# Values of both groups of a query tile together, ahead of the flip of P, in a fused attention and soft mixture-of-experts kernel

## The chip, the core and the metric

The kernel runs on one core of one Trainium2 chip. The metric is the device time of one execution in microseconds (us). Five engines work beside each other, each through its own instruction stream in order: PE (TensorE, matrix products, with its weight loads listed as PEld), DVE (VectorE), ACT (ScalarE), POOL (GpSimd) and SP, which here only issues DMAs. They meet at semaphores alone.

## The reference, cut to what matters

```python
def _attn_ref(q, k, v):                     # q, k, v: 8 x 8 heads x 576 x 64, fp32
    window = 128
    scores = 0.125 * q @ k.T
    scores = where((rel >= 0) & (rel < window), scores + slope_h * -abs(rel), -1e9)
    attn = exp(scores - max(scores)); attn = attn / (sum(attn) + 1e-9)
    return attn @ v

x = attn_out.transpose(0, 2, 1, 3).reshape(4608, 512)
logits = x @ phi                            # 4608 x 32 slots
d = softmax of logits over the tokens;  slot_input = d.T @ x
per expert (8): h = relu(slot_input @ w1[e]); slot_out = h @ w2[e]
c = softmax of logits over the slots;   out = c @ slot_out
```

## The kernel before, in words

The program has an attention part, in which the logits and the running sums of the slots are taken along, and after it the expert part. The change lies in the attention part.

**Groups and rounds.** A batch has five query tiles `t`: four of 128 rows and a tail of 64. A full tile is worked on in two groups `g` of four heads each, the tail in one of all eight, so a batch has nine groups, and there are 72 in all (`groups`). The loop `for i in range(n)` at L770 runs one round for each. Round `i` brings each of several groups one step on; for group `i` the scores are masked and reduced on DVE and go through `exp`, for group `i - 1` the result is normalised, and so on:

- `scores(i + 1)` on PE (L248 and L255, or L236 and L241 for the first tile of a batch) writes one of two PSUM banks, which `expo(i - 1)` has to have read;
- `softmax_front` on DVE: `merge` (L268, L270 or L272), `rowmax` (L290), the reciprocal for the group before (L302), `bias` (L293) and four `normalise` (L307);
- `expo` on ACT (L342): four exponentials with their row sums, into one of three buffers `p4`; it waits for the bias;
- `flip` of group `i - FLAG`, which is `i - 3`, on PE (L352): four transposes of P into the PSUM bank `pt`;
- `split` of the same group: ACT copies `pt` to SBUF (L359), and POOL cuts the copy with two selects into the part of the tile before (`pp`) and that of this tile (`pd`) (L361 and L363, for the tail L366 and L368; for the first tile of a batch there is none);
- `values` of group `i - LAG`, which is `i - 4`, on PE (L388): P times V into the PSUM bank `xp`, in which both groups of a tile meet;
- behind the second group of a tile `after_values`: ACT copies `xp` to SBUF (`x_store`, L404). `x_flip` (four transposes on PE, L409, bank `xq`) and `x_keep` (the copy of `xq` on ACT, L418) follow some rounds later.

`pd` and `pp` have two buffers each, so the copy of a group's `pt` waits for the values of the group two before it. `pt`, `xp` and `xq` have one PSUM bank each.

**What sets the order.** The order on each engine is the order in which the program issues, since the schedule is manual. `do(when, i, ...)` (L693) puts a step off to round `i` and to a place in it, and `run(when, i)` carries it out: "act" stands behind the split, "mid" and "pe" behind the scores. The steps of the slots (`logits`, `slot_flip`, `token_flip`, `slot_sum` on PE, the copies and exponentials to them on ACT) are put off in this way and lie in rounds 4 to 8 of each nine. Names such as round 0 or 3 below mean the round's number modulo 9. Since a group's values follow four rounds behind, the second group's values of the full tiles come in rounds 5, 7, 0 and 2, and the tail's in round 3.

**On PE a round before reads** scores, an `x_flip` where there is one, the flip of P, the values, and the next scores. These products use the array in different shapes: flips 128x128, values 128x64 (tail 64x64), scores 64x32 (64x128 in the first tile), logits and slot sums 128x32. On ACT a round before reads: the copy of `pt`, that of `xq`, that of `xp`, and four exponentials.

## Time and profile before

| | |
|---|---|
| median of 3 runs | 292.06 us (291.81 to 293.53) |
| profiled execution, its own time | 291.1 us |
| its span, first to last instruction | 289.4 us |
| granted TensorE clock, mean | 0.981 |
| PE busy | 273.0 us, 94% |
| PE weight loads busy | 191.7 us, 66% |
| DVE busy | 232.7 us, 80% |
| ACT busy | 204.0 us, 71% |
| POOL busy | 92.2 us, 32% |
| HBM traffic | 71.7 MB, 248 GB/s |

The profile is one execution. The rounds of the attention part fill about 16 to 222 us of the span, the expert part what follows. In a row of the timeline stand the start (us from the span's start), the time it takes, the engine, the source line, the operation, the tile written and read, shapes, a count, and in brackets the idle time of the engine ahead of it with what ended it. A PEld row is a run of weight loads, two for each fp32 product; the loads pace the products, and the gap between two PEld rows shows best where PE waits. "issue" means that nothing the profile shows ended the idle time.

### The profile page before, as it was taken

The numbers are of one execution on the slowest core, as the hardware profiler recorded it, in microseconds if no ns is written. First come the engines' busy times: TensorE is split into PE (matmuls) and PEld (weight loads), VectorE is DVE, ScalarE is ACT, GpSimd is POOL, SyncE is SP. The second block draws the span as 40 slices with busy tenths as digits, with TensorE's granted clock in tenths as the row PEclk, the third lists the DMA queues.
The fourth block names the chain that finished last, engine by engine and source line by source line (L and its number), as shares of the span: only waits on it lengthen the run. The fifth ranks groups of instructions, "written<-read, shape, count | busy, mean of one in ns | idle before, by whom it ended". The sixth has DMA issues, their size and how long they took to land.

```text
span 289.4 us, 13086 instructions
## 1 busy us (share of the span) xinstructions
PE 273.0 (94%) x5164; PEld 191.7 (66%) x5164; DVE 232.7 (80%) x729; ACT 204.0 (71%) x811; POOL 92.2 (32%) x206
## 2 busy tenths in 40 slices
PE   7399999999999999999999999999999999999981
PEld 4267777777677767776777677757777753576640
DVE  2899999999989999988999999979999533234451
ACT  2798898987988988979798887978886431023341
POOL 2025525541544244235424450634465001000000
PEclk9699999999999999999999999999999999999997
DMA  6644478978686888777777968675648779999896
GB/s 183 218 143 115 130 204 254 290 215 279 188 278 196 292 272 261 236 231 229 230 243 245 302 208 279 225 261 172 199 160 272 244 251 351 416 418 356 333 383 273
DMA packets 35025, 72.58 MB, mean 251 GB/s; under 512 B 4210, under 2 KB 15124, under 8 KB 34964
## 3 DMA queue, kind: packets, MB, share of 16 engines
q1 hardware_dynamic: 34244, 71.24, 74.2%
q8 instruction: 41, 0.67, 0.9%
q10 hardware_dynamic: 720, 0.51, 0.5%
q14 instruction: 20, 0.16, 0.2%
HBM read 62.29 MB, written 9.44 MB: 248 GB/s over the span
## 4 chain that ended last, share of the span: by engine, by line
PE 50%; DVE 40%; issue 3%; ACT 2%; POOL 1%; DMA 1%; ACTq 0%; DVEq 0%; POOLq 0%
DVE area L307 14%; DVE s L290 10%; PE xp L388 9%; DVE s L270 5%; PE pt L352 5%; PE op L947 5%; PE hp L911 5%; PE s L255 5%; PE po L968 4%; DVE s L268 3%; PE xq L409 3%; PE s L248 2%; PE lp L427 2%; PE ap L510 1%; ACT area L342 1%
## 5 line engine op out<-in xcount | busy, mean ns | idle before, releaser
L342 ACT ACTIVATE area<-s,nb 128x128 f32<-128x128 f32 x288 | 102.2, 373 | 22.0 <-DVE nb L293 20.9
L307 DVE TENSOR_SCALAR area<-area,rs 128x128 f32<-128x128 f32 x286 | 79.4, 339 | 0.6 <-DVE nb L293 0.3
L388 PE MATMUL xp<-area 128*64 128x128 f32 (+1 forms) x1104 | 75.2, 271 | 1.1 <-DMA area<-v_n 0.2
L388 PEld LDWEIGHTS xp<-area 128*64 128x64 f32 x1104 | 56.2, 136 | 16.1 <-issue 8.6
L342 ACT ACTIVATION_READ_ACCUMULATOR area<-s,nb 128x1 f32 x288 | 60.7, 211 | 0.0
L290 DVE TENSOR_REDUCE s<-s 128x4 f32<-128x512 f32 x71 | 49.5, 697 | 2.2
L359 ACT COPY area<-pt 128x512 f32<-128x512 f32 x70 | 41.9, 598 | 10.1 <-PE pt L352 9.8
L298 POOL TENSOR_SCALAR rs<-sm 128x4 f32<-128x4 f32 x70 | 13.7, 195 | 100.5 <-ACT area L342 99.7
L352 PE MATMUL pt<-unit_r,area 128*128 128x128 f32 x284 | 45.6, 283 | 0.0
L255 PE MATMUL s<-kq 64*32 64x160 f32 x1792 | 42.2, 303 | 0.0
L352 PEld LDWEIGHTS pt<-unit_r,area 128*128 128x128 f32 x284 | 31.9, 142 | 14.3 <-PE s L255 5.0
L361 POOL TENSOR_SCALAR_AFFINE_SELECT area<-area 128x512 f32<-128x512 f32 x48 | 31.2, 650 | 24.8 <-ACT area L359 22.9
L270 DVE COPY_PREDICATED s<-cst,s 128x512 f32<-128x512 int32 x48 | 32.9, 685 | 0.2 <-PE s L255 0.2
L363 POOL TENSOR_SCALAR_AFFINE_SELECT area<-area 128x512 f32<-128x512 f32 x48 | 31.4, 654 | 3.3
L255 PEld LDWEIGHTS s<-kq 64*32 64x32 f32 x1792 | 29.7, 108 | 0.6
L248 PE MATMUL s<-ramp,ones 64*32 64x320 bf16 x448 | 18.8, 311 | 5.5 <-ACT area L342 4.9
L974 DVE COPY ob<-po 128x384 f32<-128x384 f32 x24 | 12.3, 552 | 14.2 <-PE po L968 12.0
L409 PE MATMUL xq<-unit_r,area 128*128 128x128 f32 x136 | 22.0, 285 | 0.4
L404 ACT COPY area<-xp 128x512 f32<-128x512 f32 (+1 forms) x37 | 20.9, 564 | 1.9 <-PE xp L388 1.5
L418 ACT COPY area<-xq 128x512 f32<-128x512 f32 x34 | 20.7, 610 | 0.0
L974 ACT COPY ob<-po 128x384 f32<-128x384 f32 x24 | 10.3, 481 | 12.8 <-PE po L968 12.8
L409 PEld LDWEIGHTS xq<-unit_r,area 128*128 128x128 f32 x136 | 14.5, 141 | 6.2 <-issue 3.2
(167 smaller groups left out, 310.2 us busy)
## 6 DMA issues: line engine op xcount, KB each, us to landing
w<-w SPq DMA_DIRECT2D x53, 512.0 KB, 5.3
out<-ob SPq DMA_DIRECT2D x24, 384.0 KB, 4.1
kq<-q_t SPq DMA_DIRECT2D x69, 128.0 KB, 3.2
kq<-k_t SPq DMA_DIRECT2D x32, 256.0 KB, 4.1
area<-v_n SPq DMA_DIRECT2D x31, 256.0 KB, 4.4
area<-w SPq DMA_DIRECT2D x8, 512.0 KB, 4.5
area<-v_n SPq DMA_DIRECT2D x12, 128.0 KB, 3.1
kq<-w SPq DMA_DIRECT2D x3, 512.0 KB, 6.2
```

The source lines that it names most:

```text
L248: nc.tensor.matmul(s4[32 * c:32 * c + 32, 2 * par:2 * par + 2, 32 * r:32 * r + WIN], lhsT=ones[rows, 0:32], rhs=ramp[rows, h], start=True, ...
L255: nc.tensor.matmul(s4[32 * c:32 * c + 32, 2 * par + jj, 32 * r:32 * r + WIN], lhsT=qt[rows, 2 * h + jj if t == 4 else jj, 32 * r:32 * r + 32],
L270: nc.vector.copy_predicated(s4[:, :, P:2 * P], bc(mask_u, 1, 4), s4[:, :, 0:P])
L290: nc.vector.tensor_reduce(st[key]["mx"][:, us], merged(key, us), axis=AX.X, op=ALU.max, negate=True)
L307: mul(p4[:, u], p4[:, u], st[key]["rs"][:, u:u + 1])
L342: nc.scalar.activation(s["p4"][:, u], merged(key, u), AF.Exp, bias=s["nb"][:, u:u + 1], scale=SCALE, accum_out=s["sm"][:, u:u + 1],)
L352: nc.tensor.transpose(s["pt"][:, u], s["p4"][:, u], ident)
L359: copy(pa[:, us], s["pt"][:, us])
L361: nc.gpsimd.affine_select(pp[:, us], pa[:, us], [[0, m], [-1, P]], ALU.is_gt, 0.0, base=0, channel_multiplier=1)
L363: nc.gpsimd.affine_select(pa[:, us], pa[:, us], [[0, m], [1, P]], ALU.is_ge, 0.0, base=0, channel_multiplier=-1)
L388: nc.tensor.matmul(xp[D * par:D * par + D, j, 0:w], lhsT=v_slot[b, t - 1 + ph][0:rows, D * h:D * h + D], rhs=src[:, 2 * par + i] if t < 4 ...
L409: nc.tensor.transpose(xq[:, P * j:P * j + P], x_of(b, t)[:, j], ident)
```

## The change

Three things move, and nothing is added or left out.

1. The values of a tile's two groups are issued together, in the round in which the second one's were issued before. A round that closes a tile ("closing", rounds 5, 7, 0, 2 and 3) issues both groups' values, or the tail's one; the other rounds (6, 8, 1 and 4) issue none.
2. These values, and the copy of `xp` with all else in `after_values`, stand at the beginning of that round, in front of the flip of P and its copy.
3. An `x_flip` that stood behind the scores of the round behind the closing one stands there directly behind the flip of P, in front of the scores, except for some (the tiles 0 and 2 of batches 2, 4 and 6, tile 1, and the last batch).

```diff
+    def closes(key):
+        return key[2] == 1 or key[1] == 4
+
     def after_values(i, key):
         b, t, g = key
-        if not (g == 1 or t == 4):
-            return
...
-            do("pe", i + 1 + (p == 1 and late), x_flip, b, t)
+            near = b < last and (p == 3 or p in (0, 2) and not late)
+            do("flip" if near else "pe", i + 1 + (p == 1 and late), x_flip, b, t)
...
+            if i >= LAG and closes(groups[i - LAG]):
+                b, t, g = groups[i - LAG]
+                for key in [(b, t, h) for h in range(g + 1)]:
+                    values(key)
+                after_values(i, groups[i - LAG])
             if i >= FLAG:
                 flip(groups[i - FLAG])
                 split(groups[i - FLAG])
             run("act", i)
-            if i >= LAG:
-                values(groups[i - LAG])
-                after_values(i, groups[i - LAG])
+            run("flip", i)
             if i + 1 < n:
                 scores(i + 1)
...
+        values(groups[n - 5])
+        values(ga)
         token_copy(last)
         x_keep(last, 2)
         flip(gb)
...
         normalise(gd, ALL)
-        values(ga)
```

The instruction order shows it at three places. On PE, rounds 35 and 36 (numbers 8 and 0 modulo 9), from the slot sum (L510) to the scores of group 37, before:

```order
L510 MATMUL ap<-area,dn 32x512 x4
L352 MATMUL pt<-unit_r,area 128x128 x4
L388 MATMUL xp<-area 64x128 x8
L236 LDWEIGHTS ones
L236 MATMUL s_0_83<-ramp,ones 128x2x128
L236 LDWEIGHTS ones
L236 MATMUL s_0_83<-ramp,ones 128x2x128
L241 MATMUL s_0_83<-kq 128x128 x4
L409 MATMUL xq<-unit_r,area 128x128 x4
L352 MATMUL pt<-unit_r,area 128x128 x4
L388 MATMUL xp<-area 64x128 x8
```

The same place in the changed kernel:

```order
L510 MATMUL ap<-area,dn 32x512 x4
L352 MATMUL pt<-unit_r,area 128x128 x4
L236 LDWEIGHTS ones
L236 MATMUL s_0_83<-ramp,ones 128x2x128
L236 LDWEIGHTS ones
L236 MATMUL s_0_83<-ramp,ones 128x2x128
L241 MATMUL s_0_83<-kq 128x128 x4
L409 MATMUL xq<-unit_r,area 128x128 x4
L388 MATMUL xp<-area 64x128 x16
L352 MATMUL pt<-unit_r,area 128x128 x4
```

The eight values (L388) behind the first flip are gone to the next round, which has sixteen, and they stand ahead of its flip (L352).

On PE, round 39 (number 3), where the tail's values are due, between two scores, before:

```order
L248 LDWEIGHTS ones
L248 MATMUL s_1_84<-ramp,ones 32x2x160
L255 MATMUL s_1_84<-kq 32x160 x16
L352 MATMUL pt<-unit_r,area 128x128 x4
L388 MATMUL xp<-area 64x64 x16
L248 LDWEIGHTS ones
```

And in the changed kernel, the flip of the tail (round 38) now being ahead of the first rows:

```order
L248 LDWEIGHTS ones
L248 MATMUL s_1_84<-ramp,ones 32x2x160
L255 MATMUL s_1_84<-kq 32x160 x16
L388 MATMUL xp<-area 64x64 x16
L352 MATMUL pt<-unit_r,area 128x128 x4
L409 MATMUL xq<-unit_r,area 128x128 x4
L248 LDWEIGHTS ones
```

Between the scores of group 39 and those of group 40 there were the flip and the values; now there are the values, the flip and an `x_flip`.

On ACT, rounds 36 to 38, before (L359 copies `pt`, L418 `xq`, L404 `xp`, L342 is the exponential):

```order
L359 COPY area<-pt 128x512
L418 COPY area<-xq 128x512
L404 COPY area<-xp 128x512
L342 ACTIVATE area,sm<-s_0_83,nb 128x128 x4
L359 COPY area<-pt 128x512
L342 ACTIVATE area,sm<-s_1_84,nb 128x128 x4
L359 COPY area<-pt 128x512
L418 COPY area<-xq 128x512
L404 COPY area<-xp 128x512
L342 ACTIVATE area,sm<-s_0_83,nb 128x128 x4
```

And in the changed kernel:

```order
L404 COPY area<-xp 128x512
L359 COPY area<-pt 128x512
L418 COPY area<-xq 128x512
L342 ACTIVATE area,sm<-s_0_83,nb 128x128 x4
L359 COPY area<-pt 128x512
L342 ACTIVATE area,sm<-s_1_84,nb 128x128 x4
L404 COPY area<-xp 128x512
L359 COPY area<-pt 128x512
L418 COPY area<-xq 128x512
L342 ACTIVATE area,sm<-s_0_83,nb 128x128 x4
```

In the closing rounds 36 and 38 the copy of `xp` goes from behind the other two copies to the front; round 37 is the same. On DVE, POOL and SP the instructions stand in the same order as before.

## The prediction

> **What bounds the kernel now.** I read the page's busy shares and chain first, then the busy times of the rounds' stretch, then the waits, then single rounds in the timeline.
>
> ```profile
> PE 50%; DVE 40%; issue 3%; ACT 2%; POOL 1%; DMA 1%; ACTq 0%; DVEq 0%; POOLq 0%
> ```
>
> The chain lies on PE and DVE alone. The stretch of the rounds, 16 to 222 us, by engine:
>
> ```profile
> 16.00:222.00 206.00, 203.68 (x4121) 150.38 (x4120) 196.43 (x620) 176.88 (x731) 87.00 (x186) 1.00 0.72 227
> ```
>
> The columns are length, PE, PEld, DVE, ACT, POOL, clock and DMA. PE is busy for 203.7 of 206.0 us, DVE for 196.4, ACT for 176.9: PE is first, but DVE is only 7 us behind it. 206 us over about 70 rounds are 2.9 us a round. The clock is 1.00 here and plays no part. The waits:
>
> ```profile
> PEld xp L388 <- issue: 8.6, 49, 0.4
> PEld xp L388 <- POOL area L363: 1.8, 10, 0.3
> ACT area L359 <- PE pt L352: 9.8, 11, 1.5
> ACT area L404 <- PE xp L388: 1.5, 8, 0.2
> ```
>
> In front of the values PE stands still for 8.6 / 49 = 0.17 us each time with nothing to wait for. The second row says that in ten places the values already start at the moment when POOL's last select ends: there is no slack left between POOL and the values there. The last says that the copy of `xp` hardly waits today. Now a tile's rounds one by one, rounds 36 to 39 on PE's weight loads:
>
> ```profile
> 109.50 0.85 PEld L388 LDWEIGHTS xp<-area 128*64 128x64 f32 x16 [0.17 <-issue]
> 110.53 0.10 PEld L236 LDWEIGHTS <-ones 64*128 64x128 bf16 x2 [0.17 <-DVE s L268]
> ...
> 112.17 0.63 PEld L388 LDWEIGHTS xp<-area 128*64 128x64 f32 x12 [0.16 <-POOL area L363]
> ...
> 113.93 0.42 PEld L409 LDWEIGHTS xq<-unit_r,area 128*128 128x128 f32 x4 [0.25 <-issue]
> 114.32 0.47 PEld L352 LDWEIGHTS pt<-unit_r,area 128*128 128x128 f32 x4
> 114.95 0.85 PEld L388 LDWEIGHTS xp<-area 128*64 128x64 f32 x16 [0.16 <-POOL area L363]
> ...
> 116.99 0.42 PEld L352 LDWEIGHTS pt<-unit_r,area 128*128 128x128 f32 x4 [0.25 <-issue]
> 117.70 0.23 PEld L388 LDWEIGHTS xp<-area 128*64 128x64 f32 x4 [0.29 <-POOL area L366]
> 118.13 1.34 PEld L388 LDWEIGHTS xp<-area 64*64 64x64 f32 x28 [0.20 <-POOL area L368]
> 119.53 0.11 PEld L248 LDWEIGHTS <-ones 64*32 64x32 bf16 x8
> 119.56 0.53 PEld L255 LDWEIGHTS s<-kq 64*32 64x32 f32 x32
> ```
>
> The values that close tile 2 end at 109.50 + 0.85 = 110.35, those that close tile 3 at 114.95 + 0.85 = 115.80, the tail's at 118.13 + 1.34 = 119.47. So closing to closing takes 5.45 us over two rounds, and 3.67 us from tile 3 to the tail. There is a gap of 0.17 to 0.25 us wherever the shape of the array changes, and none from an x flip to a flip of P. The same rounds on ACT and POOL:
>
> ```profile
> 110.10 0.60 ACT L359 COPY area<-pt 128x512 f32<-128x512 f32 x1
> 110.56 0.62 ACT L418 COPY area<-xq 128x512 f32<-128x512 f32 x1
> 111.04 0.63 ACT L404 COPY area<-xp 128x512 f32<-128x512 f32 x1
> 111.52 0.42 ACT L342 ACTIVATE area<-s,nb 128x128 f32<-128x128 f32 x1
> ...
> 112.90 0.65 ACT L359 COPY area<-pt 128x512 f32<-128x512 f32 x1
> ...
> 116.02 0.59 ACT L359 COPY area<-pt 128x512 f32<-128x512 f32 x1
> ...
> 119.65 0.37 ACT L404 COPY area<-xp 128x256 f32<-128x256 f32 x1 [0.16 <-PE xp L388]
> ```
>
> ```profile
> 111.47 0.65 POOL L363 TENSOR_SCALAR_AFFINE_SELECT area<-area 128x512 f32<-128x512 f32 x1
> ...
> 113.62 0.63 POOL L361 TENSOR_SCALAR_AFFINE_SELECT area<-area 128x512 f32<-128x512 f32 x1 [0.27 <-ACT area L359]
> 114.33 0.63 POOL L363 TENSOR_SCALAR_AFFINE_SELECT area<-area 128x512 f32<-128x512 f32 x1
> ...
> 116.69 0.67 POOL L366 TENSOR_SCALAR_AFFINE_SELECT area<-area 128x512 f32<-128x512 f32 x1 [0.27 <-ACT area L359]
> 117.42 0.66 POOL L368 TENSOR_SCALAR_AFFINE_SELECT area<-area 64x512 f32<-64x512 f32 x1
> ```
>
> Here one sees the path that matters: exponentials 111.52, copy of `pt` 112.90, selects 113.62 to 114.96, values 114.95. And at 110.10 the copy of `pt` begins before the values of its round have ended (110.35): today ACT does not wait for the values ahead of that copy.
>
> **The change part by part.**
>
> *Fewer changes of shape.* Counted over the order of the rounds, places where the array's shape changes fall from 232 to 215: a round without values loses one, and an x flip that is left in front of values costs one. 17 changes at 0.17 to 0.25 us, the bounds of the rows, are 2.9 to 4.3 us; I take 0.20, so 3.4 us less. PE is the busiest engine, so I count it in full. Values into flip is a change that the rows hardly show; I price it like the others.
>
> *The rule on this.* The Trainium skill (TensorEngine Tiling (Array Packing), Key Properties) says that changing the tiling mode drains TensorE. The gaps of 0.17 us agree; by that rule alone the kernel gains the 3.4 us, which is the first rival.
>
> *Values ahead of the flip.* This closes a loop that was open. ACT works in order, and in a closing round `xp`, which now needs both groups' values, stands ahead of the copy of `pt`, which needs the flip behind these values; behind it come `xq`, the round's four exponentials, the next round's copy of `pt`, POOL's two selects, and the next tile's values. PE's wait in front of those values holds up the flip, scores and the rest queued behind them. How long the flip takes to release the copy, where ACT waits for it:
>
> ```profile
> 98.28 0.59 ACT L359 COPY area<-pt 128x512 f32<-128x512 f32 x1 [0.25 <-PE pt L352]
> ```
>
> ```profile
> 97.53 0.42 PEld L352 LDWEIGHTS pt<-unit_r,area 128*128 128x128 f32 x4 [0.20 <-ACT area L342]
> ```
>
> The flip's loads end at 97.95, the copy begins 0.33 later. The loop from the end of one closing round's values to the end of the next's: change 0.17, flip 0.42, release 0.33, `pt` to `xq` 0.46 (110.10 to 110.56), `xq` to the exponentials 0.48 (as 110.56 to 111.04), these 1.38 (111.52 to 112.90), copy to select 0.72, selects 113.62 to 114.96 = 1.34, release 0.05 (112.12 to 112.17), the twelve loads that read the second select 0.63. The sum is 5.98 us against 5.45, 0.53 more. The copy of `xp` hides: it begins 0.18 behind the values (119.47 to 119.65), takes 0.48, and is done at 0.66, before the flip's release at 0.92. Tile 2 to tile 3 is the stretch from a round 0 to a round 2; rounds 9 to 65 hold seven of these, 7 x 0.53 = 3.7 us. In the two other pairs with selects (5 to 7, 7 to 0) no copy of `xq` stands there, which makes the loop 0.48 shorter, 5.50, and PE has the slots' products beside it; I take nothing, at most another 3.7 us.
>
> *The tail.* From tile 3's values to the tail's lies now: 0.17, flip 0.42, release 0.33, copy to select 0.67 (116.02 to 116.69), selects to 118.08 = 1.39, release 0.05, loads 1.34: 4.37 against 3.67, 0.70 more. Before, the flip was ahead of the values, so copy and selects ran under them; now only one set of scores is there as cover. Seven times (the last batch orders its tiles otherwise) this is 4.9 us. If DVE or ACT were late there anyhow it is less; I bound it by half.
>
> *The x flips.* Those moved in front of the scores stay beside a flip, as they were, so they change no shape; the scores behind begin 0.39 us later (113.93 to 114.32). The cover is the time by which scores run ahead of DVE; if it is gone, the last rival holds. The load of V that `after_values` issues keeps its place on SP and waits for the same closing values as before: nothing.
>
> *The end of the rounds.* The flip of group 69 now stands behind two sets of values instead of ahead of one, 0.85 + 0.17 = 1.0 us later, and this chain ended here:
>
> ```profile
> 222.70 0.47 POOL L368 TENSOR_SCALAR_AFFINE_SELECT area<-area 64x256 f32<-64x256 f32 x1
> ```
>
> ```profile
> 223.57 1.60 PEld L388 LDWEIGHTS bank<-area 128*64 128x64 f32 x32
> ```
>
> The select ended at 223.17, the values began 0.40 later for other reasons, so 1.0 - 0.4 = 0.6 us; 0 to 1.0.
>
> *Sum.* 3.7 + 4.9 + 0.6 - 3.4 = 5.8 us. On the profiled execution that is 291.1 + 5.8 = 296.9, on the median, which lies 0.96 above it, 297.9; I say 298. Its own range: the loop and the tail at half give 4.3 + 0.6 - 3.4 = 1.5, so 293.6, and the other pairs' 3.7 on top give 301.6.
>
> **The rivals.**
>
> *Shapes alone (chance 0.20).* If copies and selects run early enough that PE never waits, 2.9 to 4.3 us come off: 288.7 with 3.4. For it: PE waits on little but the gaps today. Against it: the ten values that already start as POOL ends.
>
> *DVE hides the loop (0.24).* In rounds 36 and 37 DVE needs more than the loop:
>
> ```profile
> 109.74 0.69 DVE L268 COPY_PREDICATED s<-cst,fine 128x512 f32<-128x512 int32 x1
> ...
> 115.03 0.86 DVE L307 TENSOR_SCALAR area<-area,rs 128x128 f32<-128x128 f32 x4
> 115.81 0.68 DVE L270 COPY_PREDICATED s<-cst,s 128x512 f32<-128x512 int32 x1
> ...
> 117.41 1.33 DVE L307 TENSOR_SCALAR area<-area,rs 128x128 f32<-128x128 f32 x4
> ```
>
> From 109.74 to 115.81 it is 6.07 us, over 5.98. Then the 3.7 us cost nothing: 4.9 + 0.6 - 3.4 = 2.1, 294.2, no change. Against it: the normalisation takes 1.33 with a select beside it (POOL's L368 at 117.42) and 0.86 without, so where the selects come later than it, DVE's rounds shrink and hide nothing.
>
> *DVE starves (0.06).* In round 39 the scores' loads end at 119.56 + 0.53 = 120.09, and DVE's mask of them follows late:
>
> ```profile
> 121.05 0.69 DVE L270 COPY_PREDICATED s<-cst,s 128x512 f32<-128x512 int32 x1
> ```
>
> That is 0.96 later, some 0.6 more than a release like the flip's 0.33. With the tail's values 0.70 later and a flip and an x flip ahead (0.17 + 0.42 + 0.39), the scores come 1.7 later, and DVE waits 1.7 - 0.6 = 1.1. Of it 0.70 is in the sum already; 0.4 seven times is 2.8 more, 300.7. It decides once DVE idles ahead of that mask.
>
> **How the numbers follow.** About 1%, 2.9 us, is what can be told from no change. The forecast has 0.50, and it and the starving rival lie above 295: slower 0.56. No change is the hiding rival: 0.24. Faster is 0.20. To leave out no more than 2 in 10, I take 289 to 302: half of the fastest case lies below, a little of the others above.
>
> **What would show it.** Right: PE's waits in front of the values for POOL (L363, L368) grow from some 3 us to about 10, closing to closing from round 0 to 2 is near 6.0 and from 2 to the tail near 4.4; the copy of `xp` waits for PE in most closing rounds; PE's idle time under "issue" falls by some 3 us. Wrong: if these two stretches keep 5.45 and 3.67, the loop is not closed in time and the time falls under 290; if DVE shows gaps ahead of its mask, the last rival holds.

## The result and the profile after

The changed kernel takes 318.97 us (317.23 to 320.87, 6 runs) against 292.25 us (291.77 to 293.53, 6 runs): a ratio of 1.0911, 95% interval 1.0869 to 1.0953. It is slower by 26.7 us. 298 had been predicted, with a range of 289 to 302. Runs more than 1.5% above the fastest of their kernel are left out of the medians below.

The profiled execution's own time is 319.0 us, its span 317.2 us. The busy shares of its page, and the chain of waits:

```profile
PE 277.4 (87%) x5164; PEld 196.1 (62%) x5164; DVE 238.2 (75%) x729; ACT 207.7 (65%) x811; POOL 96.1 (30%) x206
...
PE 54%; ACT 19%; issue 11%; DVE 8%; POOL 7%; POOLq 0%; ACTq 0%; DVEq 0%
```

DVE's part of the chain fell from 40% to 8%; ACT's rose from 2 to 19, "issue" from 3 to 11, POOL's from 1 to 7. No engine is the bound any more; they wait for each other. The stretch of the rounds says the same (columns as in the prediction: length, PE, PEld, DVE, ACT, POOL, clock, DMA):

```profile
16.00:248.00 232.00, 207.09 (x4123) 153.91 (x4121) 201.53 (x620) 181.07 (x732) 90.77 (x186) 0.99 0.65 204
```

It is 232 us long in place of 206, so 26 of the 27 us are here. PE works 207.1 us of it, 3.4 more than before, and stands still for 24.9 where it stood still for 2.3. DVE stands still for 30.5 in place of 9.6. The clock is 0.99 and plays no part. What the engines waited for (us in total, times, longest):

```profile
ACT area L404 <- PE xp L388: 37.0, 35, 2.0
DVE s L270 <- PE s L255: 12.6, 10, 2.5
PEld L248 <- issue: 12.4, 44, 1.5
...
PE s L248 <- ACT area L342: 8.3, 13, 4.6
ACT area L359 <- PE pt L352: 7.2, 13, 1.4
...
PEld xp L388 <- POOL area L366: 7.0, 7, 1.1
...
PEld xp L388 <- issue: 4.4, 22, 0.3
PEld xp L388 <- POOL area L368: 3.9, 7, 0.6
...
PE s L248 <- DVE cs L545: 2.9, 5, 0.7
```

ACT now stops 35 times at the copy of `xp`, 37.0 us in place of 1.5. DVE stops at its mask (L270) for 12.6 in place of 0.2. PE's wait for POOL in front of the tail's values (L366, L368) is 10.9 us in place of 2.5. The scores (L248) wait for ACT's exponentials, which have to free their bank; of the 8.3 us under that name 4.6 are one wait ahead of the rounds, which the kernel before has too (4.7).

Rounds 36 to 39 of the changed kernel on PE's weight loads:

```profile
120.27 1.73 PEld L388 LDWEIGHTS xp<-area 128*64 128x64 f32 x32 [0.17 <-issue]
122.17 0.42 PEld L352 LDWEIGHTS pt<-unit_r,area 128*128 128x128 f32 x4 [0.17 <-PE xp L388]
...
124.63 0.09 PEld L248 LDWEIGHTS <-ones 64*32 64x32 bf16 x1 [0.17 <-DVE cs L544]
125.45 0.11 PEld L248 LDWEIGHTS <-ones 64*32 64x32 bf16 x7 [0.73 <-issue]
125.47 0.52 PEld L255 LDWEIGHTS s<-kq 64*32 64x32 f32 x32
126.25 1.73 PEld L388 LDWEIGHTS xp<-area 128*64 128x64 f32 x32 [0.25 <-issue]
128.15 0.42 PEld L352 LDWEIGHTS pt<-unit_r,area 128*128 128x128 f32 x4 [0.17 <-issue]
...
130.33 0.20 PEld L388 LDWEIGHTS xp<-area 128*64 128x64 f32 x4 [1.04 <-POOL area L366]
131.12 1.34 PEld L388 LDWEIGHTS xp<-area 64*64 64x64 f32 x28 [0.59 <-POOL area L368]
132.52 0.42 PEld L352 LDWEIGHTS pt<-unit_r,area 128*128 128x128 f32 x4
```

Values end at 122.00, 127.98 and 132.46. So from round 0 to round 2 it is 5.98 us (before 5.45), and from round 2 to the tail 4.48 (before 3.67). Both are what the prediction has, 5.98 and 4.37. The same rounds on ACT, then POOL, then DVE:

```profile
122.29 0.59 ACT L404 COPY area<-xp 128x512 f32<-128x512 f32 x1 [0.92 <-PE xp L388]
122.92 0.58 ACT L359 COPY area<-pt 128x512 f32<-128x512 f32 x1
123.40 0.59 ACT L418 COPY area<-xq 128x512 f32<-128x512 f32 x1
123.88 0.38 ACT L342 ACTIVATE area<-s,nb 128x128 f32<-128x128 f32 x1
...
125.16 0.23 ACT L342 ACTIVATION_READ_ACCUMULATOR area<-s,nb 128x1 f32 x1
125.25 0.62 ACT L359 COPY area<-pt 128x512 f32<-128x512 f32 x1
```

```profile
126.64 0.63 POOL L363 TENSOR_SCALAR_AFFINE_SELECT area<-area 128x512 f32<-128x512 f32 x1
```

```profile
134.55 0.69 DVE L270 COPY_PREDICATED s<-cst,s 128x512 f32<-128x512 int32 x1 [1.01 <-PE s L255]
```

The exponentials of round 36 stand behind the copies of `xp`, `pt` and `xq`, and so behind both groups' values and the flip. They end at 125.39, and at 125.45 PE goes on with scores whose first load had stopped at 124.63: these scores write the bank that the exponentials read. Behind them come the next values. This is a ring, from values to values: change of shape 0.17, flip 0.42, to the copy of `pt` 0.33, to `xq` 0.48, to the exponentials 0.48, these 1.51, to the scores 0.06, scores 0.54, change 0.26, values 1.73, together 5.98. The table of waits puts this stop of the scores down to DVE's L545, which ended at 125.45 too. But the product's own wait is for ACT; the wait for DVE belongs to the load ahead of it, which had begun at 124.63. In the changed kernel with a third buffer, described below, the same stop at the same place bears ACT's name:

```profile
123.72 0.33 PE L248 MATMUL s<-ramp,ones 64*32 64x320 bf16 x8 [0.75 <-ACT area L342]
```

The prediction's ring goes another way, over POOL's selects. They ended at 127.27. Of the 32 loads that began at 126.25, the first that reads the second select's output is the twenty-first, at about 126.25 + 1.73 x 20 / 32 = 127.33, so the selects were just in time. The two rings are equally long here to within what can be read.

The second mechanism is in the tail: there PE waits for POOL, 1.04 and 0.59. And DVE stops for 1.01 at the mask of the scores that PE makes in round 39.

With the end of the values in each closing round taken as marks, the attention part has 37 intervals of five kinds. The sums of their differences, after less before:

| from round to round | times | longer by, us |
|---|---|---|
| 0 to 2 | 7 | 5.9 |
| 2 to 3 (tail) | 7 | 6.5 |
| 3 to 5 | 7 | 3.1 |
| 5 to 7 | 8 | 4.7 |
| 7 to 0 | 8 | 4.9 |

That is 25.1 of the 27.8 us by which the span grew; the stretch behind the last mark is 3.3 longer, that ahead of the first one 0.5 shorter. The prediction has 8.6 for the first two rows and nothing for the others.

### The profile page after: what moved, and what is told of

Its sections match the earlier page's. It is cut to its first block, busy times and chain, and to the rows that moved or that the text cites. A ratio compares the mean times of both kernels' runs of the same rounds, so it can differ in the third digit from the quotient of the medians.

```text
span 317.2 us, 13050 instructions
## 1 busy us (share of the span) xinstructions
PE 277.4 (87%) x5164; PEld 196.1 (62%) x5164; DVE 238.2 (75%) x729; ACT 207.7 (65%) x811; POOL 96.1 (30%) x206
## 4 chain that ended last, share of the span: by engine, by line
PE 54%; ACT 19%; issue 11%; DVE 8%; POOL 7%; POOLq 0%; ACTq 0%; DVEq 0%
PE xp L388 14%; ACT area L342 10%; PE pt L352 5%; PE op L953 5%; PE hp L917 4%; PE s L255 4%; PE po L974 4%; PE xq L409 3%; ACT area L359 3%; ACT area L404 3%; PE lp L427 3%; PE ap L510 2%; PE s L248 2%; DVE area L307 2%; POOL area L366 2%
## 5 line engine op out<-in xcount | busy, mean ns | idle before, releaser
L342 ACT ACTIVATE area<-s,nb 128x128 f32<-128x128 f32 x288 | 102.4, 377 | 8.3 <-DVE nb L293 6.6
L307 DVE TENSOR_SCALAR area<-area,rs 128x128 f32<-128x128 f32 x286 | 81.2, 345 | 0.8 <-DVE nb L293 0.3
L388 PE MATMUL xp<-area 128*64 128x128 f32 (+1 forms) x1104 | 67.6, 268 | 7.7 <-POOL area L366 4.8
L388 PEld LDWEIGHTS xp<-area 128*64 128x64 f32 x1104 | 56.6, 136 | 19.9 <-POOL area L366 7.0
L342 ACT ACTIVATION_READ_ACCUMULATOR area<-s,nb 128x1 f32 x288 | 61.9, 215 | 0.0
L361 POOL TENSOR_SCALAR_AFFINE_SELECT area<-area 128x512 f32<-128x512 f32 x48 | 34.0, 708 | 58.1 <-ACT area L359 39.2
L352 PE MATMUL pt<-unit_r,area 128*128 128x128 f32 x284 | 47.9, 292 | 1.4 <-DVE area L307 1.1
L359 ACT COPY area<-pt 128x512 f32<-128x512 f32 x70 | 41.5, 592 | 9.3 <-PE pt L352 7.2
L404 ACT COPY area<-xp 128x512 f32<-128x512 f32 (+1 forms) x37 | 20.2, 545 | 37.2 <-PE xp L388 37.0
L255 PE MATMUL s<-kq 64*32 64x160 f32 x1792 | 43.9, 309 | 0.4 <-issue 0.4
L270 DVE COPY_PREDICATED s<-cst,s 128x512 f32<-128x512 int32 x48 | 33.0, 688 | 12.9 <-PE s L255 12.6
L352 PEld LDWEIGHTS pt<-unit_r,area 128*128 128x128 f32 x284 | 31.4, 144 | 18.1 <-issue 9.4
L363 POOL TENSOR_SCALAR_AFFINE_SELECT area<-area 128x512 f32<-128x512 f32 x48 | 31.9, 665 | 3.3
L248 PE MATMUL s<-ramp,ones 64*32 64x320 bf16 x448 | 19.0, 316 | 11.2 <-ACT area L342 8.3
L248 PEld LDWEIGHTS <-ones 64*32 64x32 bf16 x448 | 8.1, 89 | 21.0 <-issue 12.4
L418 ACT COPY area<-xq 128x512 f32<-128x512 f32 x34 | 20.4, 601 | 0.0
L409 PEld LDWEIGHTS xq<-unit_r,area 128*128 128x128 f32 x136 | 15.5, 145 | 7.7 <-ACT area L418 6.8
```

The lines of the kernel that those rows point to most:

```text
L248: nc.tensor.matmul(s4[32 * c:32 * c + 32, 2 * par:2 * par + 2, 32 * r:32 * r + WIN], lhsT=ones[rows, 0:32], rhs=ramp[rows, h], start=True, ...
L255: nc.tensor.matmul(s4[32 * c:32 * c + 32, 2 * par + jj, 32 * r:32 * r + WIN], lhsT=qt[rows, 2 * h + jj if t == 4 else jj, 32 * r:32 * r + 32],
L270: nc.vector.copy_predicated(s4[:, :, P:2 * P], bc(mask_u, 1, 4), s4[:, :, 0:P])
L307: mul(p4[:, u], p4[:, u], st[key]["rs"][:, u:u + 1])
L342: nc.scalar.activation(s["p4"][:, u], merged(key, u), AF.Exp, bias=s["nb"][:, u:u + 1], scale=SCALE, accum_out=s["sm"][:, u:u + 1],)
L352: nc.tensor.transpose(s["pt"][:, u], s["p4"][:, u], ident)
```

## The experiments

Theory at the beginning: the ring over ACT and POOL, closed because the values stand in front of the flip. Rivals: the x flips in front of the scores, and the gathering of both groups' values in one round, wherever it stands.

### Which part of the change

The x flips of the change alone, in the kernel before:

```diff
-            do("pe", i + 1 + (p == 1 and late), x_flip, b, t)
+            near = b < last and (p == 3 or p in (0, 2) and not late)
+            do("flip" if near else "pe", i + 1 + (p == 1 and late), x_flip, b, t)
...
             run("act", i)
+            run("flip", i)
```

> The kernel before, with the x flips of the change alone (directly behind the flip of P in the round behind the closing one). Loop theory (the cost of the change is a closed loop PE to ACT to POOL to PE, made by putting the values ahead of the flip): nothing is closed here, 290 to 294 us. Rival, x flips: scores that come 0.39 us later starve DVE, and most of the 27 us is here, 305 us or more. Rival, gathering: 290 to 294 us as well.

Measured: 291.99, ratio 0.9991 (0.9969 to 1.0013). The rival of the x flips is out.

All but the x flips, in the changed kernel:

```diff
-            near = b < last and (p == 3 or p in (0, 2) and not late)
-            do("flip" if near else "pe", i + 1 + (p == 1 and late), x_flip, b, t)
+            do("pe", i + 1 + (p == 1 and late), x_flip, b, t)
...
-            run("flip", i)
```

> The changed kernel with the x flips back behind the scores. Loop theory: the loop is whole, 312 to 321 us. Rival, x flips: near 292 us. Rival, gathering (two groups' values in one round load PE unevenly, so scores come late in that round, and the even rounds cannot make it good): 312 to 321 us.

Measured: 319.73, ratio 1.0967 (1.0893 to 1.1041). The x flips cost nothing and save nothing. The whole loss lies with the values.

Now the kernel before with each group's values in their own round, but in front of the flip, so that nothing is gathered:

```diff
+            if i >= LAG:
+                values(groups[i - LAG])
+                after_values(i, groups[i - LAG])
             if i >= FLAG:
                 flip(groups[i - FLAG])
                 split(groups[i - FLAG])
             run("act", i)
-            if i >= LAG:
-                values(groups[i - LAG])
-                after_values(i, groups[i - LAG])
```

> The kernel before, with each group's values in the round that they had, but in front of the flip of P; nothing is gathered. Loop theory: the loop closes in every round that has selects: change 0.17, flip 0.42, release 0.33, copy to select 0.72, selects 1.34, release 0.05, loads 0.63 make 3.66 us a round against 2.9, in about 49 rounds, so some 37 us more: 320 to 335 us. Rival, gathering: only the array's shape changes more often (268 times for 232, 36 x 0.2 us), 297 to 301 us.

Measured: 336.83, ratio 1.1554 (1.1387 to 1.1720), 1.8 over the range of the loop theory. Without any gathering the position in front of the flip costs even more, since every round has the ring then. Its waits name POOL:

```profile
PEld xp L388 <- POOL area L361: 17.0, 22, 1.5
PEld xp L388 <- POOL area L363: 13.4, 32, 0.8
```

And the values gathered with the flip between them: the first group's in front of it, the second's and the copy of `xp` behind it, again against the kernel before:

```diff
+            closing = i >= LAG and closes(groups[i - LAG])
+            if closing and groups[i - LAG][2]:
+                values(groups[i - LAG - 1])
             if i >= FLAG:
                 flip(groups[i - FLAG])
                 split(groups[i - FLAG])
             run("act", i)
-            if i >= LAG:
+            if closing:
                 values(groups[i - LAG])
                 after_values(i, groups[i - LAG])
...
+        values(groups[n - 5])
         token_copy(last)
```

> Both groups' values in the closing round, the first group's in front of the flip of P, the second's and the copy of xp behind it, the x flips as before. Loop theory: what is ahead of the flip has been ready for long, the copy of pt waits for no select, nothing is closed; 252 changes of shape for 232 are 4 us: 292 to 298 us. Rival, gathering: the round's load on PE is as uneven as in the changed kernel: 310 to 320 us.

Measured: 304.81, ratio 1.0455 (1.0386 to 1.0524). Neither expectation holds: about half of the loss is left with the second group's values behind the flip. So there is more than one cause. The next two runs take two of them apart. First gathering alone, the flip first and both groups' values behind it:

```diff
+            closing = i >= LAG and closes(groups[i - LAG])
             if i >= FLAG:
                 flip(groups[i - FLAG])
+            if closing:
+                b, t, g = groups[i - LAG]
+                for key in [(b, t, h) for h in range(g + 1)]:
+                    values(key)
+            if i >= FLAG:
                 split(groups[i - FLAG])
             run("act", i)
-            if i >= LAG:
-                values(groups[i - LAG])
+            if closing:
                 after_values(i, groups[i - LAG])
...
+        values(groups[n - 5])
         token_copy(last)
```

> PE makes the flip of P first and then the values of both groups together; ACT copies P^T behind that, the flips of x stay behind the scores as in the kernel before. There are 203 changes of shape on PE, against 232 before and 252 in the run with the flip between the two groups' values. The loop theory (the values wait for POOL's selects and the flip waits for the values): nothing of the flip waits for POOL now, 286 to 292. A second theory, which the run with the flip between the groups suggests (what PE does ahead of ACT's copy of P^T holds up ACT, and with it the exponentials that free the bank for the next scores; here the copy still waits for the first group's values, whose buffer it overwrites): the time of that run less 49 changes of 0.2, 304.8 - 9.8 = 295, so 292 to 300. A third (gathering both groups' values costs by itself, wherever they stand): 304 or more.

Measured: 300.59, ratio 1.0297 (1.0263 to 1.0331). It lies in none of the three ranges, 0.6 over the second. The loop theory alone is out: gathering costs 8.3 us with nothing in front of the flip, although there are 29 changes of shape fewer than in the kernel before.

Then position alone, only the closing group's values in front and nothing gathered:

```diff
+            closing = i >= LAG and (groups[i - LAG][2] == 1 or groups[i - LAG][1] == 4)
+            if closing:
+                values(groups[i - LAG])
+                after_values(i, groups[i - LAG])
             if i >= FLAG:
                 flip(groups[i - FLAG])
                 split(groups[i - FLAG])
             run("act", i)
-            if i >= LAG:
+            if i >= LAG and not closing:
                 values(groups[i - LAG])
-                after_values(i, groups[i - LAG])
```

> The kernel before with only the closing group's values and the copy of x ahead of the flip; the first group's values stay in their own round behind its flip, so nothing is gathered. If what the changed kernel lost over the flip-first kernel (319.0 - 300.6 = 18.4) comes from the closing group's values standing ahead of the flip: 292.3 + 18 = 310, so 304 to 316. If both groups' values have to stand there (the longer stop of ACT behind both): 295 to 303.

Measured: 312.57, ratio 1.0689 (1.0609 to 1.0770). Position alone costs 20.4. The two, 8.3 and 20.4, add up to 28.7, near the 26.7 of the change. But the intervals of the three traces, in us over the kernel before, show that it is no sum of parts:

| from round to round | changed kernel | gathering alone | position alone |
|---|---|---|---|
| 0 to 2 | 5.9 | 4.6 | 5.6 |
| 2 to 3 (tail) | 6.5 | -2.3 | 6.5 |
| 3 to 5 | 3.1 | -0.9 | 2.3 |
| 5 to 7 | 4.7 | 5.1 | 3.9 |
| 7 to 0 | 4.9 | 2.3 | 2.4 |

From round 0 to 2 and from 5 to 7 either of the two alone costs about as much as both; the loss in the tail is position alone.

### ACT's order or PE's, and POOL's selects

In the changed kernel ACT copies `xp` ahead of `pt`. One run swaps the two on ACT and leaves PE as it is:

```diff
-                after_values(i, groups[i - LAG])
             if i >= FLAG:
                 flip(groups[i - FLAG])
                 split(groups[i - FLAG])
+            if i >= LAG and closes(groups[i - LAG]):
+                after_values(i, groups[i - LAG])
```

> The changed kernel with one swap on ACT: the copy of P^T goes first and the copy of x behind it; PE's order is that of the changed kernel. If the loss comes from PE's order (the flip behind the values), ACT still waits for the flip, which ends about when the copy of x would have ended: 316 to 320. If it comes from ACT's order (the copy of x, 0.59, ahead of the copy of P^T in 36 rounds, at most 21): 300 to 308.

Measured: 329.43, ratio 1.1282 (1.1236 to 1.1328). Not ACT's order: the swap costs another 10 us, outside both expectations. The copy of `xp` had run while ACT waited for the flip; behind the copy of `pt` that cover is gone. From tile 2 to tile 3 of batch 3 it is 6.47 in place of 5.98, and the 0.49 are one copy's step on ACT (0.48); the tail, whose ring runs over POOL, keeps its 4.48.

Then POOL's second select was left out, in the changed kernel and, as a control, in the kernel before:

```diff
-            nc.gpsimd.affine_select(
-                pa[:, us], pa[:, us], [[0, m], [1, P]], ALU.is_ge, 0.0, base=0, channel_multiplier=-1)
```

> The changed kernel without the second of POOL's two selects in each split (the diagonal blocks are left unmasked, a part of the computation is left out). The loop theory: POOL's 0.70 leaves every stretch in which the values wait for POOL. For the stretches from round 0 to 2 and from 2 to the tail that is 14 x 0.70 = 10, so 309; if the other three kinds of stretch run through POOL too, 35 x 0.70 = 24, so 295 at the lowest: 295 to 311. If POOL is not in what was lost (ACT held up by PE's order alone): 316 or more.

Measured: 311.60, ratio 1.0679 (1.0643 to 1.0714), 7.4 less than the changed kernel and 0.6 over the range of the loop theory.

> The kernel before without the second of POOL's two selects (the same part of the computation left out), as the control. Values there wait for POOL rarely and for fractions of a us, so both theories have 290 to 292.5. If this run gains as much as the one of the changed kernel, the selects cost the same in both and say nothing of the loss.

Measured: 288.14, ratio 0.9873 (0.9836 to 0.9911), 4.1 less, more than expected. So the loss shrinks by only 3.3 us, not 10. This difference of two gains says little of POOL's part, since DVE too became 9.9 us less busy in the kernel before. The traces of the changed kernel are clearer: without the second select the seven tails take 27.4 us in place of 30.9 together, while the seven stretches from round 0 to 2 take 44.2 in place of 44.1. With POOL's time taken off, the ring through the scores' bank is still there.

### A false trail: DVE beside POOL

DVE is busy for 242.3 us in the flip-first kernel and 232.7 in the kernel before, and the difference, 9.6, is near the loss of 8.3. Most of it, 7.3, lies in one group, the normalisation: here the kernel before, the flip-first kernel, and the flip-first kernel with one select (behind the bar: busy us, mean ns of one).

```profile
L307 DVE TENSOR_SCALAR area<-area,rs 128x128 f32<-128x128 f32 x286 | 79.4, 339 | 0.6 <-DVE nb L293 0.3
```

```profile
L307 DVE TENSOR_SCALAR area<-area,rs 128x128 f32<-128x128 f32 x286 | 86.7, 365 | 0.8 <-ACT area L404 0.3
```

```profile
L307 DVE TENSOR_SCALAR area<-area,rs 128x128 f32<-128x128 f32 x286 | 76.2, 329 | 1.8 <-DVE nb L293 0.3
```

So a contention theory was formed: selects that come later fall beside the normalisation and stretch it. Two runs test it. The first moves the selects alone, by putting the exponentials ahead of the copy of `pt` in the kernel before; the second takes one select out of the flip-first kernel.

```diff
             if i >= FLAG:
                 flip(groups[i - FLAG])
+            if i:
+                expo(new)
+            if i >= FLAG:
                 split(groups[i - FLAG])
...
-            if i:
-                expo(new)
```

> The kernel before with one swap on ACT and nothing else moved: in each round the exponentials of the newest scores go ahead of the copy of P^T, so that the copy, and POOL's selects behind it, come about 1.4 later beside DVE's work; PE's order is that of before and no wait for PE is added. Contention theory (a select beside DVE's normalise makes it longer, beside DVE's maximum it costs nothing; in the kernel before the selects start 0.27 behind the start of the maximum, in the middle): DVE is busy for 238 or more in place of 232.7, and the time is 296 to 305. Waiting theory (what costs is ACT waiting for PE): nothing is added, 289 to 293.

Measured: 388.49, ratio 1.3229 (1.3110 to 1.3349). Both expectations fall, and the run says nothing on contention: the selects come so late there that hardly a piece of the normalisation meets one, and it takes 283 ns in the mean, less than anywhere else. A chain nobody had counted closes instead. Its waits:

```profile
POOL area L361 <- ACT area L359: 150.4, 47, 5.1
ACT area L342 <- DVE nb L293: 110.0, 54, 4.5
...
PEld pt L352 <- ACT area L359: 19.1, 18, 2.3
```

ACT stops at its exponentials for DVE's bias, and the copy of `pt` stands behind them; the next flip needs the bank that this copy frees, POOL needs the copy, and so do the values. It is the fault of the change again, on another engine: what others need stands behind an instruction that waits.

> The kernel with the flip first and the values of both groups together behind it, without the second of POOL's selects (the diagonal blocks are left unmasked, a part of the computation is left out). To be held against the same omission in the kernel before, 288.1. Contention theory: the 8.3 by which the flip-first kernel lost come from selects beside normalise; with one select most of that goes, 287 to 292. Waiting theory (ACT's copy waits for the first group's values, whose buffer it overwrites): that wait stays, 288.1 + 8.3 = 296.4, so 294 to 299.

Measured: 299.97, ratio 1.0250 (1.0188 to 1.0313). DVE is busy for 230.9 there, 11.4 less than with both selects, and the time falls by 0.6, to 1.0 over the range of the waiting theory. Contention is real but not what the flip-first kernel loses by.

### A third buffer, and the values a round later

The flip-first kernel waits here:

```profile
ACT area L359 <- PE xp L388: 21.8, 25, 1.8
```

ACT's copy of `pt` writes the buffer that the first group's values read, now a round longer. A third buffer for `pa` and `pp` takes that wait away (one weight buffer fewer makes the room):

```diff
-NW = 36
+NW = 35
...
-    area = cpool.tile([P, 19, HW], F32, name="area")
+    area = cpool.tile([P, 21, HW], F32, name="area")
...
-    pas, pps = [halves(i) for i in (6, 8, 7)], [halves(i) for i in (7, 9)]
+    pas, pps = [halves(i) for i in (6, 8, 19)], [halves(i) for i in (7, 9, 20)]
...
-        i = number[key] % 2 if number[key] < n - 1 else 2
+        i = number[key] % 3
...
-        pa, pp = pas[i], pps[i % 2]
+        pa, pp = pas[i], pps[i]
```

> The control: the kernel before with the same third buffer and one weight buffer fewer. Its copy of P^T waits for values hardly ever (the largest wait of that copy is for the flip, 9.8 us), so 290.5 to 293.5 by both theories; whatever it moves has to be taken off the other two runs.

Measured: 292.10, ratio 1.0005 (0.9973 to 1.0038). The buffer by itself changes nothing.

> The kernel with the flip first and the values of both groups together behind it, given a third buffer for P^T and its selected copy, so that ACT's copy of P^T no longer waits for the first group's values (room is made by one weight buffer fewer, 35 in place of 36). Waiting theory (in the flip-first kernel ACT waits 21.8 us for values whose buffer it overwrites, with exponentials queued behind): that wait goes; what stays is 29 fewer changes of shape, 292.3 - 29 x 0.2 = 286.5, so 285 to 293. Rival (what costs is that in a closing round PE has two groups' values between the flip and the next scores, whatever ACT does): 297 to 302.

Measured: 298.26, ratio 1.0229 (1.0195 to 1.0263). The buffer's wait was worth 2.3; 6.2 of gathering are left over the control, in the rival's range.

> The changed kernel with the same third buffer. Waiting theory: the flip itself stands behind the values there, and the copy of x too, so ACT waits as long as before and the buffer changes nothing: 316 to 320. If the buffers of P^T are what holds the changed kernel, it falls like the flip-first kernel: 300 to 310.

Measured: 316.57, ratio 1.0846 (1.0812 to 1.0880). It falls by 2.4 as well; the rest, 18.3 over the flip-first kernel with the same buffer, is position.

With three buffers the values can come one round later, so that their selects were issued a round earlier, all else as in the changed kernel:

```diff
-            if i >= LAG and closes(groups[i - LAG]):
-                b, t, g = groups[i - LAG]
+            lag = LAG + 1 if i < n - 7 else LAG
+            if i >= lag and closes(groups[i - lag]):
+                b, t, g = groups[i - lag]
```

> The changed kernel with the third buffer for P^T, and the values one round later (but for the last seven rounds): they still stand together in front of the flip, and ACT still has to wait for them and for the flip, but POOL's selects on which they depend were issued a round earlier, so the values never wait for POOL. To be held against the changed kernel with the third buffer alone, 316.6. If the ring that runs from the values over the flip, ACT's copy and POOL's selects to the next values is what the position in front costs: down to the flip-first kernel with the third buffer and two times what the first group's values cost in front of the flip, 298.3 + 2 x 4.2 = 306.7, so 302 to 310. If ACT's stop behind the values and the flip is enough by itself: 313 to 318.

Measured: 307.22, ratio 1.0506 (1.0450 to 1.0563). Without the ring through POOL half of what the position costs is gone, 316.57 - 307.22 = 9.4 us; the other half is still there, 307.22 - 298.26 = 9.0. The place shows in the trace. Rounds with three buffers, then with three buffers and the values later, from the values of tile 2 of batch 3 over those of tile 3 to the tail's:

```profile
118.59 1.73 PEld L388 LDWEIGHTS xp<-area 128*64 128x64 f32 x32 [0.17 <-issue]
...
123.72 0.11 PEld L248 LDWEIGHTS <-ones 64*32 64x32 bf16 x7 [0.74 <-issue]
...
124.52 1.73 PEld L388 LDWEIGHTS xp<-area 128*64 128x64 f32 x32 [0.25 <-issue]
...
128.49 0.20 PEld L388 LDWEIGHTS xp<-area 128*64 128x64 f32 x4 [0.93 <-POOL area L366]
129.27 1.34 PEld L388 LDWEIGHTS xp<-area 64*64 64x64 f32 x28 [0.59 <-POOL area L368]
```

```profile
116.83 1.73 PEld L388 LDWEIGHTS xp<-area 128*64 128x64 f32 x32 [0.17 <-issue]
...
121.96 0.11 PEld L248 LDWEIGHTS <-ones 64*32 64x32 bf16 x7 [0.73 <-issue]
...
122.76 1.73 PEld L388 LDWEIGHTS xp<-area 128*64 128x64 f32 x32 [0.25 <-issue]
...
126.05 1.60 PEld L388 LDWEIGHTS xp<-area 128*64 128x64 f32 x32 [0.25 <-issue]
```

To the tail it is 130.61 - 126.25 = 4.36 us in the first and 127.65 - 124.49 = 3.16 in the second, 1.20 less. Six tails come a round later (the last is among the last seven rounds and keeps its place), and together they are 7.3 of the 9.4 us shorter. From tile 2 to tile 3 it is 5.93 in both, with the same stop in front of the scores, 0.74 and 0.73. So POOL's selects decide almost only in the tail; the 5.93 are the ring through ACT's exponentials and the scores' bank.

Last, the 6.2 us of gathering: ACT's stop at the copy of `xp` or PE's order? The copy of `xp` was moved behind the exponentials in the flip-first kernel with three buffers:

```diff
-            if closing:
-                after_values(i, groups[i - LAG])
...
             if i:
                 expo(new)
+            if closing:
+                after_values(i, groups[i - LAG])
```

> The kernel with the flip first, the values of both groups behind it and the third buffer (298.3), with ACT's copy of x moved behind the exponentials of the round, so that no exponential waits for values any more; PE's order is the same. If the 6.2 that gathering still costs come from ACT stopping at the copy of x (20.9 us of waits there, exponentials queued behind it): 290 to 294. If they come from PE (two groups' values between one flip and the next scores, so that scores come late in one round and early in the next): 297 or more.

Measured: 303.69, ratio 1.0436 (1.0342 to 1.0530). No exponential waits for values there, and it is slower, not faster. That does not clear ACT's stop, for the late copy brings a wait of its own:

```profile
PE xp L388 <- ACT area L404: 8.8, 7, 1.8
```

`xp` has one bank, and the tail's values, one round behind those of tile 3, have to wait until the copy has read it. The intervals take the two apart. Over the same kernel with the copy ahead, the seven tails are 9.3 us longer. From round 0 to 2 it is 3.3 us shorter, 38.4 in place of 41.8, and the kernel before with the third buffer has 38.1. Nearly all that gathering costs in this stretch goes with ACT's stop. With the copy ahead, the trace shows the stop of the scores there:

```profile
117.09 0.33 PE L248 MATMUL s<-ramp,ones 64*32 64x320 bf16 x8 [0.84 <-ACT area L342]
```

It is the ring over the scores' bank again, which ACT here enters by the copy of `xp`: values, copy, exponentials, scores, next values. With the copy behind the exponentials the scores don't stop there. From 5 to 7 the copy's move takes 1.5 us off and from 7 to 0 it adds 1.3; there 2.6 and 3.6 us over the control are left. That PE's rounds are uneven (two groups' values in one, none in the next, on an engine that had 2.3 us to spare in 206) agrees with this rest, but no run shows it by itself, and it stays open. Nor was a second bank for `xp` tried, which would let the copy come late without holding up the tail.

No variant that does the whole computation beat the kernel before; the nearest are the x flips alone and the third buffer alone, both the same.

## Why the prediction was wrong

The sign was right and the size was not: +5.8 us predicted, +26.7 measured. Point by point:

**Round 0 to 2 and the tail: right in size, half right in path.** 5.98 and 4.37 were predicted, 5.98 and 4.48 measured. For the tail the path was right: it runs over POOL's selects, and giving the selects a round takes 7.3 us off six tails. For round 0 to 2 the path named was not the one that decides: the length stays 5.93 when POOL is taken out of it. The ring that decides shares the first half (flip, `pt`, `xq`, exponentials) and goes on over the scores' bank. That the sums agree is chance. The prediction never followed the exponentials to the bank that they free, though the scores' wait for `expo` is part of how the kernel was described.

**"I take nothing" for the pairs 5 to 7 and 7 to 0: wrong, and the largest error.** They grew by 9.6 us, and the pair 3 to 5, which the prediction doesn't name, by 3.1: 12.7 us together. The bound given was 3.7. The reason for the "nothing" was that the ring is 0.48 shorter there and PE has the slots' products as cover. The predicted ring is not even needed for the loss in the two pairs: gathering alone, with nothing ahead of the flip, makes them 7.4 us longer, and position alone 6.3. And the slots' products (`dp`, `ap`) are no cover: those that wait need an ACT step that stands behind the same stop. The x flip (`xq`) waits for such a step too, half of the time from 7 to 0 and half from 0 to 2. Waits that were 1.9, 0.3 and 0.3 us before are now:

```profile
PEld xq L409 <- ACT area L418: 6.8, 11, 0.9
...
PEld dp L494 <- ACT lg L476: 3.3, 7, 0.7
...
PEld ap L510 <- ACT dn L503: 2.6, 6, 0.4
```

**"I count it in full", -3.4 us for fewer changes of shape: wrong.** A saving on PE counts only while PE is the bound, and the same sum closes a ring in which PE waits. PE's busy time rose by 3.4 us in the rounds and its idle time by 22.6. What the prediction asked to see, some 3 us less idle under "issue", is there in front of the values (8.6 to 4.4) and comes back in front of the scores (5.0 to 12.4). With 29 fewer changes the flip-first kernel with three buffers is still 6.2 slower, so the credit did not show even with nothing ahead of the flip. Nor is there a gap "wherever" the shape changes: behind the tail's values the next loads begin 0.06 us later (119.47 to 119.53 in the prediction's rows). By the Trainium skill (TensorEngine Tiling (Array Packing), Key Properties) the array drains at a change; the gaps of 0.17 agree with it, the gain does not follow from it.

**Gathering taken as free: wrong.** The flip-first run puts 8.3 us on it, 6.2 without the buffer's wait. The prediction priced no consequence of two groups' values in one round but the ring ahead of the flip; that ACT's exponentials stand behind a copy that now needs both groups' values was left out, and from round 0 to 2 this alone is 3.3 us.

**The x flips at nothing: right**, 0.9991. **Shapes alone** and **DVE hides the loop**: out, since DVE idles 20.9 us more in the rounds. **DVE starves**: it had 0.06 and its place was right, since DVE waits 1.01 at that mask in the rounds shown, where 1.1 was worked out; but it came on top of the rest, and the 300.7 that it was to give came from the same short sum. **The end of the rounds**, 0.6, was too small: the stretch behind the last mark takes 71.1 us in place of 67.8, 3.3 more. In part that is the flip of group 69, which now lies behind the mark; the rest was not followed up.

The loss comes apart like this, from run to run, in one order of taking the steps (another order would share it out otherwise, as the table of intervals shows): 292.1 (third buffer) to 298.3, gathering behind the flip, 6.2; to 307.2, the values in front of the flip without waits for POOL, 9.0 (with them the x flips' place and the later round, which this step also changes); to 316.6, POOL's selects, 9.4, of which 7.3 are tails; to 319.0, the buffer, 2.4.

## What to carry to other kernels

Before an instruction is moved ahead of another on an in-order engine, write down every ring that runs through the pair, the ones through shared banks and buffers as well as the ones through data, and compare each with the time between two rounds; where two rings are equally long, shortening one shows nothing. Cover that itself depends on the stopped engine is no cover, and a saving on the bounding engine, 17 changes of shape here, did not show in a change that makes this engine wait. When a run that takes a wait away is slower, look for the wait that it put in its place before the first is cleared: the late copy of `xp` gained 3.3 us in one stretch and lost 9.3 in another.

## What was unexpected of the hardware

DVE's normalisation is stretched by a select on POOL beside it, its maximum is not. In the changed kernel four pieces took 1.68 us with the selects of 129.55 and 130.35 running, and 0.88 with none:

```profile
129.47 1.68 DVE L307 TENSOR_SCALAR area<-area,rs 128x128 f32<-128x128 f32 x4
...
131.78 0.70 DVE L290 TENSOR_REDUCE s<-s 128x4 f32<-128x512 f32 x1
...
132.66 0.88 DVE L307 TENSOR_SCALAR area<-area,rs 128x128 f32<-128x128 f32 x4
```

```profile
129.55 0.72 POOL L366 TENSOR_SCALAR_AFFINE_SELECT area<-area 128x512 f32<-128x512 f32 x1 [1.56 <-ACT area L359]
...
130.35 0.72 POOL L368 TENSOR_SCALAR_AFFINE_SELECT area<-area 64x512 f32<-64x512 f32 x1
```

Over all pieces, those that hardly overlap a select take 0.28 us and those that overlap it by more than 0.4 us 0.65 to 0.68, in every kernel of this study that has such; the maximum, which reads PSUM, takes 0.70 in either case. The Trainium skill (SBUF — State Buffer, SBUF: two separate sides) has a port pair that VectorE (in some of its modes) and GpSimd share, which one instruction holds to its end; the longer pieces, 0.65 to 0.68 us beside selects that take 0.64 in the median, agree with it. The runs add that it did not set the time of the flip-first kernel: 11.4 us of DVE taken off it were worth 0.6, while 9.9 taken off the kernel before, where DVE is next to the bound, were worth 4.1.
